# One core: batch 2's K transposed by TensorE, pairwise PV normalisation in tile 0, single banks in tile 1

## The chip, the core and the metric

The kernel runs on one core of a Trainium2 chip. A core has TensorE (PE in the profile; PEld is its weight load), VectorE (DVE), ScalarE (ACT), GpSimd (POOL) and SyncE (SP), each with an instruction queue of its own that is worked off in order, and 16 DMA engines that all of the core's transfers share. SP issues DMAs into a hardware queue (q1 in the profile), POOL into a software queue (q0). The metric is device time in microseconds (us); smaller is better.

## What is computed

Causal attention with a window of 64 positions over 8 batches, 8 heads, 576 positions, head dimension 64, and then a feed-forward block on the 4608 tokens:

```python
scores = scale * q @ k.T          # masked to 0 <= i - j < 64
attn = softmax(scores)
x = (attn @ v) as (4608, 512)     # tokens x (heads * head_dim)
h = x @ w_in                      # (4608, 2048)
g = h * clip(h + 3, 0, 6) / 6
out = g @ w_out                   # (4608, 512)
```

## The kernel before

**Tiles and stages.** The feed-forward part works on nine tiles of 512 tokens. Tile T has a stage 1 (`s1`, L524: 16 chunks of four 128x512 matmuls, L531, each chunk followed by `gate`, L536, which is a ScalarE activation, L538, and a VectorE product, L539) and a stage 2 (`s2`, L561: four output blocks of 16 matmuls, L568, a ScalarE copy to `osb`, L574, and a store). Tile T needs the attention output `xT` of batch T, because a batch has 576 tokens and a tile has 512; the last 64 positions of a batch are called its remainder.

**Attention of the next batch is woven into the stages.** Heads are taken in four pairs. `SS` (L630) computes the scores of a pair (ten small matmuls, L354, two exps on ScalarE, L362, one mask product on VectorE, L372). `N_` (L613) multiplies the probabilities with V, whose extra column of ones gives the sums (PV, L384 to L395), and VectorE divides head by head (L403 and L406). `X_` (L618) transposes the result into `xT` on TensorE and copies it with ScalarE (L422); `xt_dma` (L474) does the same with a DMA transpose on SP. `TT` (L621) transposes Q and K of a pair on TensorE, `RR` (L626) the remainder's. `rest_s`, `rest_n`, `rest_x` (L427 to L468) do attention of batch 0's remainder.

**The order is written out by hand.** `run` or `go` lets a stage go on by one block, and the calls between put attention work there. After stage 1 of tile 0, L760 to L798 interleave stage 2 of tile 0 (all four output blocks a quarter at a time, so that each quarter of w_out may land late) with batch 1's attention and batch 0's remainder. From tile 1 on `stage_` (L800) does it, with the tables that `pieces` (L820) returns: p1 holds what follows which chunk of stage 1, p2 what follows which block of stage 2. In tiles 1 and 2 stage 1 begins with four chunks held open, pair by pair, with the last two `X_` of the batch in between.

**PSUM** has eight banks: `st0` and `st1` of two banks each (scores, and other uses), `o`, `acc`, `h0` and `h1`. `s1_bank` (L494) says where a chunk of stage 1 goes. In tiles 1 and 2 the first four chunks take `st0` and `st1` as double banks with one gate over both halves.

**Loads.** Q, K and V of a batch pass a staging tile (`qst`, `kst`, `vst`, one buffer each), are cast to bf16 by POOL and then transposed. Batches 0 and 1 load Q and K in 1 KB runs (`LoadsForPE`, L101) and transpose on TensorE. Batches 2 to 7 load blocks of 256 B runs on SP (`load_blocks`, L88) and transpose by DMA on SP: batch 2 in eight transposes by pair (L280), the later ones in two whole ones (L272). The weights come on POOL's queue. V of batch 1 comes on SP, head by head (`load_v_by_head`, L121), made to wait for the third piece of w_out (L729). Casts and DMA issues of POOL stand in one order, L642 to L657 and L709 to L744 and L842 to L847. At most eight transfers of one queue are outstanding, since each issue waits for the landing of the eighth before it.

Of the kernel before, what the change touches and what calls it, by code (L numbers as in the profile page):

```python
# [9 lines left out]
F32 = mybir.dt.float32  # L10
# [14 lines left out]
def kernel(  # L25
# [53 lines left out]
    def load_v(b, vst, h0, h1):  # L79
        out = []  # L80
        for h in range(h0, h1):
            out.append(nc.sync.dma_start(
                out=vst[:, 0 : KB - 1, h, :],
                in_=v[b, h, 0:SM, :].rearrange("(k p) d -> p k d", p=P),
            ))
        return out

    def load_blocks(t, src, b, kbs, tail=0):  # L88
        out = []
        for kb in kbs:  # L90
# [3 lines left out]
            out.append(nc.sync.dma_start(  # L94
# [5 lines left out]
    class LoadsForPE:  # L100
        def __init__(self, b):  # L101
            self.b = b
            self.qst = stage.tile([P, H, R * D], F32, name="qst", tag="qst")
# [4 lines left out]
        def main(self, i, h0, h1):  # L108
            nc.gpsimd.dma_start(
# [4 lines left out]
        def rest(self):  # L114
            for i, src in enumerate((q, k)):
                nc.gpsimd.dma_start(
                    out=self.rst[i * SR : (i + 1) * SR, :, :],
# [3 lines left out]
    def load_v_by_head(b):  # L121
        vst = stage.tile([P, KB, H, D], F32, name="vst", tag="vst")
        ins = load_blocks(vst, v, b, (KB - 1,), SR) + load_v(b, vst, 0, H)
        return vst, ins

    def load_for_dma(b):
        sts, ins = [], []
        for n, src in (("qst", q), ("kst", k), ("vst", v)):
# [112 lines left out]
    class Batch:  # L241
# [28 lines left out]
        def transpose_by_dma(self):  # L270
            for n, T in ((qn_all, self.QT), (kn_all, self.KT)):
# [4 lines left out]

        def transpose_pairs_by_dma(self):
            for g in range(NG):
                for n, T in ((qn_all, self.QT), (kn_all, self.KT)):
                    nc.sync.dma_start_transpose(  # L280
                        out=T[:, g, :].rearrange("d (k s) -> d k s", s=P),
                        in_=n[:, g, :, :, :].rearrange("p k h d -> p (k h d)"),
                    )
# [8 lines left out]
        def cast_rest(self, st, copy):  # L292
            self.rn = consts.tile([P, H, D], BF16, name=f"rn{self.b}")
            copy(out=self.rn[:], in_=st[2][:])

        def rest_t(self, tr):
# [13 lines left out]
            return evac  # L310

# [100 lines left out]

    def xt_pe(bt, g, tr):
# [29 lines left out]
    def rest_n(bt, u):  # L443
# [8 lines left out]
        for h in range(2):  # L452
            ov = st[0:SR, h, 0 : NG * VW].rearrange("p (g w) -> p g w", w=VW)
            rec = small.tile([P, KB], F32, name="rec")
            nc.vector.reciprocal(out=rec[0:SR, 0:NG].unsqueeze(2), in_=ov[:, :, D:VW])
            nc.vector.tensor_tensor(
                out=opr[0:SR, :, h, :], in0=ov[:, :, 0:D],
# [433 lines left out]
```

## Time and profile before

| what | value |
|---|---|
| median of 8 runs | 313.96 us (313.03 to 314.9) |
| the profiled execution | 313.85 us |
| its span in the profile | 312.1 us |
| stage 1 of tile 0 starts at | 18.74 us |
| stage 2 of tile 0 starts at | 34.30 us |
| tiles 1, 2, 3 start at | 57.57, 91.70, 125.61 us |
| HBM read, written | 36.70 MB, 9.44 MB |

The span is the time from the first to the last instruction; some 1.75 us of the execution lie around it. The page has one row with each engine's busy time, 40 slices of the span, the DMA queues, the chain of work that ended last, and groups of instructions by line. The timeline lists an engine's instructions in order of time, with the idle time before each and what ended it in brackets. In the chain that ended last TensorE has the share to be seen here:

```profile
PE 86%; DMA 5%; DVE 3%; ACT 3%; issue 1%; SPq 1%; POOL 0%; POOLq 0%
```

### The profile page before, as it was taken

What the parts mean: (1) busy time and instruction counts of PE and PEld (TensorE: products, weight loads), DVE (VectorE), ACT (ScalarE), POOL (GpSimd) and SP (SyncE); (2) the same over time, 40 slices, a digit from 0 to 9 for tenths busy, and PEclk for the clock granted to TensorE, in tenths of its full rate; (3) what the DMA queues carried; (4) which work ended last, traced back from release to release, by engine and by line L of the source; (5) the groups of instructions that cost most, each with busy time, mean ns of one, the idle gap of its engine ahead of it and who ended that gap; (6) DMA issues with size and microseconds to landing.
All of it is one profiled execution on the core that took longest, in us unless ns stands there. A gap on an engine that the chain in (4) does not pass through costs nothing.

```text
span 312.1 us, 5616 instructions
## 1 busy us (share of the span) xinstructions
PE 302.2 (97%) x2162; PEld 148.2 (47%) x2162; DVE 174.7 (56%) x334; ACT 177.5 (57%) x264; POOL 92.9 (30%) x137
## 2 busy tenths in 40 slices
PE   8889998899999999999999999999999999999995
PEld 3445444544654455445544554455445544444442
DVE  4659546385636754578347844785377527306700
ACT  3848754587627853796169615871588157317611
POOL 5876615372055043415600660075000000000000
PEclk9999999999999999999999999999999999999999
DMA  7999999998899999999999999999900630010011
GB/s 248 209 220 241 245 200 205 206 244 174 187 205 213 266 201 213 220 227 210 191 250 199 203 192 245 213 206 187 250 3 0 129 93 0 34 69 34 0 69 67
DMA packets 147579, 52.80 MB, mean 169 GB/s; under 512 B 136384, under 2 KB 142528, under 8 KB 147552
## 3 DMA queue, kind: packets, MB, share of 16 engines
q1 hardware_dynamic: 141920, 44.18, 70.4%
q0 software_dynamic: 5360, 8.00, 12.7%
q8 instruction: 17, 0.28, 0.4%
q10 hardware_dynamic: 272, 0.26, 0.2%
q14 instruction: 10, 0.08, 0.1%
HBM read 36.70 MB, written 9.44 MB: 148 GB/s over the span
## 4 chain that ended last, share of the span: by engine, by line
PE 86%; DMA 5%; DVE 3%; ACT 3%; issue 1%; SPq 1%; POOL 0%; POOLq 0%
PE acc L568 19%; PE o L568 18%; PE h L531 17%; PE st L531 8%; PE o L531 6%; PE acc L531 6%; PE st L354 4%; DMA win<-in_moe_w_in_dram 2%; PE h L384 2%; DVE gT L539 2%; PE h L568 1%; DMA qst<-in_q_dram 1%; PE h L389 1%; ACT pT L362 1%; DMA vst<-in_v_dram 1%
## 5 line engine op out<-in xcount | busy, mean ns | idle before, releaser
L531 PEld LDWEIGHTS <-win 128*128 128x128 bf16 x576 | 55.1, 98 | 66.6 <-issue 1.6
L568 PEld LDWEIGHTS <-gT 128*128 128x128 bf16 x576 | 52.5, 98 | 57.0 <-issue 0.5
L568 PE MATMUL o<-wout,gT 128*128 128x512 bf16 x272 | 65.7, 380 | 0.0
L568 PE MATMUL acc<-wout,gT 128*128 128x512 bf16 x272 | 63.8, 379 | 0.0
L531 PE MATMUL h<-xT,win 128*128 128x512 bf16 x264 | 63.3, 379 | 0.0
L362 ACT ACTIVATE pT<-st 128x768 bf16<-128x768 f32 x64 | 48.8, 808 | 13.7 <-PE st L354 13.6
L539 DVE SCALAR_TENSOR_TENSOR gT<-t,st 128x512 bf16<-128x512 bf16 (+1 forms) x26 | 20.7, 810 | 57.2 <-ACT t L538 57.0
L538 ACT ACTIVATE t<-h,half 128x512 bf16<-128x512 f32 x66 | 44.7, 691 | 8.4 <-PE h L531 7.9
L539 DVE SCALAR_TENSOR_TENSOR gT<-t,h 128x512 bf16<-128x512 bf16 x66 | 44.6, 685 | 7.8 <-ACT t L538 7.7
L372 DVE TENSOR_TENSOR pT<-pT,mask 128x1536 bf16<-128x1536 bf16 x28 | 28.3, 1009 | 21.1 <-ACT pT L362 21.1
L258 POOL CAST qn<-qst 128x512 bf16<-128x512 f32 x24 | 15.9, 703 | 72.1 <-DMA qst<-in_q_dram 51.6
L574 ACT COPY osb<-acc 128x512 f32<-128x512 f32 x17 | 10.0, 587 | 42.8 <-PE acc L568 42.6
L531 PE MATMUL st<-xT,win 128*128 128x512 bf16 x128 | 30.9, 379 | 1.1 <-DMA win<-in_moe_w_in_dram 0.7
L574 ACT COPY osb<-o 128x512 f32<-128x512 f32 x17 | 10.0, 588 | 29.9 <-PE o L568 29.9
L406 DVE TENSOR_TENSOR opg<-h,rec 128x320 bf16<-128x320 f32 x50 | 24.6, 492 | 1.7
L531 PE MATMUL o<-xT,win 128*128 128x512 bf16 x92 | 23.6, 379 | 0.3 <-DVE gT L539 0.3
L538 ACT ACTIVATE t<-st,half 128x512 bf16<-128x512 f32 (+1 forms) x26 | 20.1, 785 | 6.3 <-PE st L531 6.2
L531 PE MATMUL acc<-xT,win 128*128 128x512 bf16 x92 | 23.6, 379 | 0.0
L248 POOL CAST V<-vst 128x512 bf16<-128x512 f32 (+1 forms) x14 | 16.6, 1185 | 16.6 <-DMA vst<-in_v_dram 10.6
L384 PEld LDWEIGHTS <-pT 128*128 128x128 bf16 x256 | 17.5, 97 | 7.8 <-DVE opg L406 0.9
L258 POOL CAST kn<-kst 128x512 bf16<-128x512 f32 x24 | 15.8, 699 | 17.0 <-DMA kst<-in_k_dram 14.1
L354 PE MATMUL st<-QT,KT 64*128 64x192 bf16 (+2 forms) x312 | 17.5, 230 | 0.9 <-ACT KT L322 0.5
(111 smaller groups left out, 282.8 us busy)
## 6 DMA issues: line engine op xcount, KB each, us to landing
out_dram<-osb SPq DMA_DIRECT2D x32, 256.0 KB, 2.5
qst<-in_q_dram SPq DMA_DIRECT2D x28, 256.0 KB, 4.8
kst<-in_k_dram SPq DMA_DIRECT2D x27, 256.0 KB, 5.4
vst<-in_v_dram SPq DMA_DIRECT2D x24, 256.0 KB, 5.6
vst<-in_v_dram SPq DMA_DIRECT2D x23, 128.0 KB, 3.9
win<-in_moe_w_in_dram POOLq DMA_DIRECT2D x4, 512.0 KB, 8.4
wout<-in_moe_w_out_dram POOLq DMA_DIRECT2D x4, 512.0 KB, 12.6
qst<-in_q_dram POOLq DMA_DIRECT2D x2, 512.0 KB, 11.7
```

The lines of the kernel that those rows point to most:

```text
L248: copy(out=self.V[:, 0 : KB - 1, h0:h1, 0:D], in_=vst[:, 0 : KB - 1, h0:h1, :])
L258: pcopy(out=n[:, g, 0 : KB - 1, :, :].rearrange("p k h d -> p k (h d)"), in_=s[:, 0 : KB - 1, 2 * g : 2 * g + 2, :].rearrange("p k h d -> ...
L354: nc.tensor.matmul(st[:, h, o0 : o0 + n], lhsT=bt.KT[h * D : (h + 1) * D, g, k0 : k0 + P], rhs=bt.QT[h * D : (h + 1) * D, g, q0 : q0 + n], ...
L362: nc.scalar.activation(out=pT[:, :, 2 * u : 2 * u + 2, 0:QW], in_=st[:, :, 0:w].rearrange("p h (k w) -> p h k w", k=2), func=EXP, scale=scale,
L372: nc.vector.tensor_tensor(out=pT[:, :, :, 0:QW], in0=pT[:, :, :, 0:QW], in1=mask[:].rearrange("p (h k) w -> p h k w", h=2), op=MULT,)
L384: nc.tensor.matmul(ob, lhsT=pT[:, h, qb, 0:P], rhs=V[:, qb, 2 * g + h, :], start=True, stop=(qb == 0),)
L406: nc.vector.tensor_tensor(out=opgs[bt.b, g][:, 0:nb, h, :], in0=ov[:, :, 0:D], in1=rec[:, 0:nb].unsqueeze(2).to_broadcast([P, nb, D]), op= ...
L531: nc.tensor.matmul(hT, lhsT=win16[:, g, fc * P : (fc + 1) * P], rhs=xT[:, g, t0 : t0 + TB], start=(g == 0), stop=(g == NG - 1),)
L538: nc.scalar.activation(out=t1[:], in_=hT, func=RELU, bias=half[:], scale=1.0 / 6.0)
L539: nc.vector.scalar_tensor_tensor(out=out, in0=t1[:], scalar=1.0, in1=hT, op0=MIN, op1=MULT,)
L568: nc.tensor.matmul(accs[ts], lhsT=gT[:, fc, ts * P : (ts + 1) * P], rhs=wout16[:, fc, :], start=(fc == 0), stop=(fc == NFC - 1),)
L574: acopy(out=osb[:], in_=accs[ts])
```

## The change

What it does, part by part:

- **Q and K of batch 2.** Q is loaded as before in 256 B runs, then transposed by one whole DMA transpose. K is loaded in 1 KB runs by SP, in two transfers and one for the remainder, cast by POOL and transposed by TensorE in tile 1: pairs 0, 1, 2 after chunks 10, 12, 14 of stage 1, pair 3 and the remainder (`rest_tk`) after the first two blocks of stage 2. The eight DMA transposes by pair go.
- **V of batch 1** is loaded by POOL's queue instead of SP's, and its explicit wait for w_out goes. Q of batch 2 waits for V's third head instead.
- **Batch 1's remainder** of Q and K is loaded before the first piece of w_out, cast before the second and third, and transposed on TensorE before the last chunk of tile 0's stage 1.
- **Tile 0's stage 2** is ordered anew: both halves of a pair's scores together and earlier, PV of the four pairs at the end in `st0` and `st1` in turn, each pair normalised by one reciprocal and one product (`pv_pair`; the remainder likewise). Batch 0's remainder of Q and K is cast by VectorE and that of V by ScalarE, not by POOL.
- **Stage 1 of tile 1** takes single banks in turn out of six (`turn`), with one gate per chunk from the first on. Tile 2 keeps its double banks for four chunks and takes other banks after them.
- **Batch 3** gets `xT` by DMA transposes like the later batches, not by `X_`. Its casts and transposes are moved in the tables, and its scores start three chunks earlier.

The diff, cut to its core:

```diff
+        def __init__(self, b, eng):
+            self.b, self.eng = b, eng
+            self.qst = None if b > 1 else stage.tile([P, H, R * D], F32, name="qst", tag="qst")
...
-            nc.gpsimd.dma_start(
+            self.eng.dma_start(
...
+        def rest(self, which=(0, 1)):
+            for p, i in enumerate(which):
+                src = (q, k)[i]
+                self.eng.dma_start(
+                    out=self.rst[p * SR : (p + 1) * SR, :, :],
...
-        ins = load_blocks(vst, v, b, (KB - 1,), SR) + load_v(b, vst, 0, H)
+        ins = load_blocks(vst, v, b, (KB - 1,), SR, nc.gpsimd) + load_v(b, vst, 0, H, nc.gpsimd)
...
+        def rest_tk(self, tr):
+
+            for g in range(NG):
+                nc.tensor.transpose(
+                    out=tr[:, g * SR : (g + 1) * SR],
+                    in_=self.rn[0:SR, 2 * g : 2 * g + 2, :].rearrange("p h d -> p (h d)"),
+                    identity=ident[0:SR, 0:SR],
+                )
+            acopy(
+                out=self.KT[:, :, SM:S], in_=tr[:, 0 : NG * SR].rearrange("d (g s) -> d g s", s=SR),
+            )
 
         def main_t(self, g, i, tr, copy=None):
 
@@ -410,6 +417,19 @@
 
         return norm
 
+    def pv_pair(bt, g, u):
+        t = ps_st.tile([P, 2, 512], F32, name=f"st{u}")
+        for h in range(2):
+            pv(bt, g, h, t[:, h, :])
+        ov = t[:, :, 0 : KB * VW].rearrange("p h (k w) -> p h k w", w=VW)
+        rec = small.tile([P, 2, KB], F32, name="rec2")
+        nc.vector.reciprocal(out=rec[:].unsqueeze(3), in_=ov[:, :, :, D:VW])
+        opgs[bt.b, g] = opool.tile([P, KB, 2, D], BF16, name="opg")
+        nc.vector.tensor_tensor(
+            out=opgs[bt.b, g][:].rearrange("p k h d -> p h k d"), in0=ov[:, :, :, 0:D],
+            in1=rec[:].unsqueeze(3).to_broadcast([P, 2, KB, D]), op=MULT,
+        )
...
-        for h in range(2):
-            ov = st[0:SR, h, 0 : NG * VW].rearrange("p (g w) -> p g w", w=VW)
-            rec = small.tile([P, KB], F32, name="rec")
-            nc.vector.reciprocal(out=rec[0:SR, 0:NG].unsqueeze(2), in_=ov[:, :, D:VW])
-            nc.vector.tensor_tensor(
-                out=opr[0:SR, :, h, :], in0=ov[:, :, 0:D],
-                in1=rec[0:SR, 0:NG].unsqueeze(2).to_broadcast([SR, NG, D]), op=MULT,
-            )
-
-    def rest_x(bt, u):
-        tr = ps_st.tile([P, 2, 1024], BF16, name=f"st{u}")[:, 0, :]
+        ov = st[0:SR, :, 0 : NG * VW].rearrange("p h (g w) -> p h g w", w=VW)
+        rec = small.tile([P, 2, KB], F32, name="rec2")
+        rec = rec[0:SR, :, 0:NG]
+        nc.vector.reciprocal(out=rec.unsqueeze(3), in_=ov[:, :, :, D:VW])
+        nc.vector.tensor_tensor(
+            out=opr[0:SR].rearrange("p g h d -> p h g d"), in0=ov[:, :, :, 0:D],
+            in1=rec.unsqueeze(3).to_broadcast([SR, 2, NG, D]), op=MULT,
+        )
+
+    def rest_x(bt, tr):
...
+        if T == 1:
+            return turn()
+        if T == 2:
+            if fc in (8, 9):
+                return ps_st.tile([P, 2, 512], F32, name=f"st{fc % 2}")[:, 0, :]
+            if fc in (6, 7, 12, 13):
+                return (ps_o, ps_acc)[fc % 2].tile([P, 512], F32, name=("o", "acc")[fc % 2])[:]
+            return h_bank()[:]
...
+    def turn(tr=False):
+        i = turns[0] % 6
+        turns[0] += 1
+        shape, dt = ([P, 1024], BF16) if tr else ([P, 512], F32)
+        if i < 2:
+            return ps_h.tile(shape, dt, name=h_name())[:]
+        if i < 4:
+            return (ps_o, ps_acc)[i - 2].tile(shape, dt, name=("o", "acc")[i - 2])[:]
+        return ps_st.tile([P, 2, shape[1]], dt, name=f"st{i - 4}")[:, 0, :]
...
+        if T == 1:
+            hTs = [turn() for fc in range(4)]
+            for gs in first:
+                for fc in range(4):
+                    mms(fc, hTs[fc], gs)
+                yield
+            for fc in range(4):
+                mms(fc, hTs[fc], (NG - 1,))
+                gate(gT[:, fc, :], hTs[fc], [P, TB])
+                yield
+        elif first:
...
+    ld = LoadsForPE(1, nc.gpsimd)
     ld.main(0, 0, 4)
     ld.main(1, 0, 4)
     w_in.append(load_w_in(1536, 2048, 0, NG))
+    ld.rest()
     w_out = [load_w_out(0, 4)]
...
-    ld.rest()
     ld.main(0, 4, 8)
     ld.main(1, 4, 8)
...
+    bt.cast_rest(st, pcopy)
     w_out += [load_w_out(4 * i, 4 * i + 4) for i in (1, 2)]
     rst0, rvst0 = load_rest_of_first()
+    cast_pairs(bt, st, 4, 4)
     w_out.append(load_w_out(12, 16))
     vst1, insv = load_v_by_head(1)
-    for x in insv:
-        after(x, w_out[2], "the weights go first")
-    bt.cast_rest(st, pcopy)
-    cast_pairs(bt, st, 4, 4)
-    bt0.cast_rest((None, None, rst0), pcopy)
-    run(m, 11)
+    run(m, 12)
     TT(bt, 0, oa_tr)
     run(m, 2)
     TT(bt, 1, oa_tr)
+
+    def st_tr(u):
+        t = ps_st.tile([P, 2, 1024], BF16, name=f"st{u}")
+        return iter((t[:, 0, :], t[:, 1, :]))
+
+    run(m, 1)
+    RR(bt, st_tr(0))
     run(m)
 
-    pcopy(out=bt0.V[SR:P, KB - 1, :, 0:D], in_=rvst0[SR:P, :, :])
     bt.cast_v_end(vst1, pcopy)
     for g in range(NG):
         bt.cast_v(vst1, 2 * g, 2 * g + 2, pcopy)
-    st2, _ = load_for_dma(2)
-
...
+    st2, ins2 = load_for_dma(2, (0,))
+    after(ins2[0], insv[3], "the values go first")
+    ld = LoadsForPE(2, nc.sync)
+    ld.main(1, 0, 4)
+    ld.main(1, 4, 8)
+    ld.rest((1,))
...
-    S1_(0, 0, 0)
-    S1_(1, 0, 1)
+    def SS1_(g):
+        S1_(g, 0, 0)
+        S1_(g, 1, 1)
+
+    go()
+    SS1_(0)
     go(2)
-    RR(bt, st_tr(0))
+    SS1_(1)
     go()
-    S1_(0, 1, 1)
+    TT(bt, 2, st_tr(0))
     go()
-    S1_(1, 1, 0)
-    TT(bt, 2, st_tr(1))
+    TT(bt, 3, st_tr(1))
     go(2)
-    TT(bt, 3, st_tr(0))
+    SS1_(2)
+    go(3)
+    bt0.cast_rest((None, None, rst0), vcopy)
+    RR(bt0, st_tr(0))
     go()
-    S1_(2, 0, 1)
+    SS1_(3)
+    acopy(out=bt0.V[SR:P, KB - 1, :, 0:D], in_=rvst0[SR:P, :, :])
+    go(2)
+    rest_s(bt0, 0)
+    go(2)
+    rest_n(bt0, 1)
+    pv_pair(bt, 0, 0)
     go()
-    S1_(2, 1, 0)
-    go()
-    S1_(3, 0, 1)
-    go()
-    S1_(3, 1, 0)
-    go()
-    RR(bt0, st_tr(1))
-    go()
-    rest_s(bt0, 0)
-    go()
-    rest_n(bt0, 1)
-    go()
-    N_(bt, 0, st_pair(0))
-    go()
-    N_(bt, 1, oa)
-    rest_x(bt0, 0)
-    go()
-    two = st_tr(1)
-    X_(bt, 0, two)
-    X_(bt, 1, two)
-    N_(bt, 2, oa)
-    N_(bt, 3)
+    pv_pair(bt, 1, 1)
+    X_(bt, 0, oa_tr)
+    rest_x(bt0, next(oa_tr))
+    pv_pair(bt, 2, 0)
+    pv_pair(bt, 3, 1)
+    X_(bt, 1, st_tr(0))
 
...
-            X_(Batch(T), 2, oa_tr)
+            X_(Batch(T), 2, oa_tr if T == 2 else st_tr(0))
             run(m, 1)
-            X_(Batch(T), 3, oa_tr)
+            X_(Batch(T), 3, oa_tr if T == 2 else st_tr(1))
...
-            return p1, {
-                1: [f(SS, 0)], 2: [f(SS, 1)], 4: [f(N_, 0), f(SS, 2)], 6: [f(X_, 0)], 7: [f(N_, 1), f(SS, 3)],
-                9: [f(X_, 1)], 11: [f(N_, 2)], 13: [f(N_, 3)],
-            }
-        if bt.b == 3:
-            return {13: [f(SS, 0)]}, {
-                0: [f(SS, 1)], 3: [f(N_, 0), f(SS, 2)], 5: [f(X_, 0)], 6: [f(N_, 1), f(SS, 3)],
-                8: [f(X_, 1)], 9: [f(N_, 2)], 11: [f(X_, 2)], 12: [f(N_, 3)], 14: [f(X_, 3)],
+            def k_t(g, tr, copy):
+                return lambda: bt.main_t(g, 1, tr() if tr else turn(True), copy)()
+
+            return {
+                10: [k_t(0, None, acopy)], 12: [k_t(1, None, vcopy)], 14: [k_t(2, None, acopy)],
+            }, {
+                0: [k_t(3, h_tr, vcopy)], 1: [lambda: bt.rest_tk(h_tr())],
+                2: [f(SS, 0)], 4: [f(SS, 1)], 6: [f(N_, 0), f(SS, 2)], 8: [f(N_, 1), f(SS, 3)],
+                9: [f(X_, 0)], 11: [f(N_, 2)], 12: [f(X_, 1)], 14: [f(N_, 3)],
             }
...
-    bt2.cast_for_dma(st2, (0, 1))
+    bt2.cast_for_dma((*st2, None), (0,))
+    vst2 = stage.tile([P, KB, H, D], F32, name="vst", tag="vst")
+    load_blocks(vst2, v, 2, range(3), SR)
+    bt2.transpose_by_dma((0,))
+    load_blocks(vst2, v, 2, range(3, KB), SR)
+    for h in (0, 4):
+        bt2.cast_qk(ld.tiles, 1, h, 4, pcopy)
+    bt2.cast_rest(ld.tiles, pcopy, SR)
     for u0, osb in held:
         nc.gpsimd.dma_start(out=out[u0 : u0 + P, :], in_=osb[:])
-    bt2.cast_for_dma(st2, (2,))
-    bt2.transpose_pairs_by_dma()
+    bt2.cast_for_dma((None, None, vst2), (2,))
...
+            (p2 if T == 1 else p1).setdefault(6, []).append(
                 lambda bt=nxt, sts=sts: bt.cast_for_dma(sts)
             )
-            p2.setdefault(6 if T < 3 else 12, []).append(lambda bt=nxt: bt.transpose_by_dma())
+            p2.setdefault(8 if T == 1 else 12, []).append(lambda bt=nxt: bt.transpose_by_dma())
...
```

## The prediction

> **What bounds the kernel now.** I read the page's busy row first, then its slices, then a table of stages cut at each tile's first matmul, then the matmul timeline inside the stages that stand out.
>
> ```profile
> PE 302.2 (97%) x2162; PEld 148.2 (47%) x2162; DVE 174.7 (56%) x334; ACT 177.5 (57%) x264; POOL 92.9 (30%) x137
> PEclk9999999999999999999999999999999999999999
> DMA  7999999998899999999999999999900630010011
> ```
>
> TensorE is busy 97% of 312.1 us at full granted clock, so time goes away only where TensorE waits or has less to do. The DMA engines are full until about 230 us, so each moved transfer needs its landing checked.
>
> ```profile
> 34.30:57.57 23.27, 21.44 (x217) 11.23 (x215) 11.64 (x26) 12.57 (x20) 9.96 (x18) 1.00 1.19 205
> 57.57:72.83 15.26, 14.85 (x80) 6.65 (x77) 10.94 (x19) 10.72 (x15) 10.23 (x16) 1.00 1.22 228
> 91.70:107.10 15.40, 15.10 (x85) 7.10 (x84) 8.87 (x12) 11.91 (x18) 5.98 (x8) 1.00 1.10 235
> 107.10:125.61 18.51, 18.51 (x179) 10.43 (x178) 10.16 (x22) 9.82 (x16) 7.17 (x11) 1.00 1.15 205
> 125.61:157.40 31.79, 31.79 (x234) 15.63 (x233) 19.34 (x36) 18.53 (x28) 12.48 (x16) 1.00 1.15 214
> 253.00:280.60 27.60, 27.60 (x130) 12.48 (x129) 11.01 (x16) 13.34 (x20) 0.00 (x0) 1.00 0.11 40
> ```
>
> Columns: stretch, its length, then busy PE, PEld, DVE, ACT, POOL. The stretches are stage 2 of tile 0, stage 1 of tile 1, stages 1 and 2 of tile 2, tile 3, tile 7. A tile without attention takes 27.60 (13.8 a stage); one with a batch's attention and xT by DMA 31.79. Tile 1 takes 57.57 to 91.70, 34.13; tile 2 33.91. The first row holds 13.8 of matmuls and about 6.4 of attention, counted from row pitches: scores 0.54 a pair (0.44 of them issued before 34.30), PV 0.49 a pair, four transposes 0.22, five 0.28, the remainder's three steps 0.8. That is 20.2 of 23.27: **3.1 us of waits** (modelled matmul ends hide part of them from the busy column). The timeline of TensorE shows the largest, with the releaser in brackets:
>
> ```profile
> 49.02 0.29 PE L431 MATMUL st<-QT,KT 64*128 64x64 bf16 x8 [0.57 <-DVE KT L308]
> 50.51 0.44 PE L448 MATMUL st<-V,pTr 128*64 128x65 bf16 x8 [0.23 <-DVE pTr L438]
> 56.32 0.44 PE L417 MATMUL st<-ident,opg 128*128 128x128 bf16 x5 [0.94 <-ACT xT L422]
> 63.93 2.15 PE L531 MATMUL st<-xT,win 128*128 128x512 bf16 x8 [0.30 <-DVE gT L539]
> ```
>
> **Tile 0's tail.** The batch-1 remainder transpose (0.22) moves ahead of the last stage-1 chunk, so stage 2 begins 0.22 later relative to 33.86, where TensorE leaves stage 1 now: 34.1. It needs `rn`, which POOL casts after the two 128 KB loads that now go before `w_out`. w_in's last piece lands at 29.6; the two loads took 1.6 together behind w_out's first piece (32.3 to 33.9), so 31.2, cast by 31.9, wanted at 33.0. w_out's first piece moves back by the same 1.6 to 33.9, wanted at 34.1: covered by 0.2. Pieces two and three are issued behind that cast, 31.9 instead of 27.9, while the queue is occupied until 36.7; they still land near 39.05 and 41.8, against 39.4 and 45 wanted.
>
> The walk, TensorE's clock in us: block 35.0; score pair 0 waits until ScalarE frees its bank from the remainder's K copy (35.3), 35.85; two blocks and pair 1, 38.1; block and transposes of pair 2, 39.4; block, pair 3's, 40.75; two blocks and score pair 2, 43.0; three blocks, 45.6. Batch 0's remainder cast now stands on DVE behind the mask product: ScalarE's two exps end at 44.4, the mask (1.0) at 45.4, the cast at 46.0. No row has this cast; DVE's 128x256 and 128x512 copies take 0.29 and 0.68, POOL's same cast 0.62; I take 0.6. Wait 0.4. Remainder transpose and block, 47.1; score pair 3, two blocks, 49.4; remainder scores and two blocks, 51.35. Both waits shown at 49.02 and 50.51 are covered by these blocks. Remainder PV, 51.7; PV 0, 52.2; block, 53.1; PV 1, 53.55.
>
> Here DVE sets the pace. It now normalises a pair at once. Its rows:
>
> ```profile
> 52.45 0.20 DVE L403 RECIPROCAL rec<-st 128x5 f32<-128x5 f32 x1 [0.29 <-PE st L395]
> 52.67 0.49 DVE L406 TENSOR_TENSOR opg<-st,rec 128x320 bf16<-128x320 f32 x1
> 51.19 0.42 DVE L456 TENSOR_TENSOR opr<-st,rec 64x256 bf16<-64x256 f32 x1
> ```
>
> From 256 to 320 elements costs 0.07, so 640 cost 0.84 and, with 0.21 for the reciprocal, a pair 1.0 instead of 1.28. Remainder done at 52.7, pair 0 53.75, pair 1 54.75. The xT transposes of pair 0 follow at 53.85 to 54.1, remainder transpose 54.35, PV 2 54.85, PV 3 55.35. Those of pair 1 now sit in score bank 0, which DVE is still reading for pair 2 until 55.9: they run 56.0 to 56.3. So a DVE release takes the place of the 0.94 on ScalarE. Tile 1 starts at 56.3 instead of 57.57: **-1.3**.
>
> V of batch 1 leaves SP (nine issues, 41.90 to 49.3) for POOL, behind w_out's last piece (its issue moves from 34.33 to about 37.9, lands 46.2, wanted 48.5). Nine POOL issues at the 0.71 of the `rst` loads are 6.4 us; two wait for landings at 46.2 and 46.9. POOL's casts of V queue behind them, and batch 2's Q loads on SP wait for V's third head.
>
> The Trainium skill speaks against this: "DMA: Bandwidth & Descriptors", section "SWDGE vs HWDGE vs iDMA", gives plain transfers to SP or ACT and only casting or irregular ones to GpSimd. Its row on SP: now the last V cast runs at 51.81. On POOL the nearest row is `rst`, 128 KB in 256 B runs, whose landings lie 0.5 to 1.1 apart; I take 0.8, as SP's 256 B blocks arrive (256 KB every 1.1 to 1.4) and the full engines price both alike. Fourth item (V's third head) at 49, Q's first bytes 1.7 later, then both queues share. In 66 to 72 us the software queue's out stores took 53% of the engines' time beside SP's 60%, so about half each: nine loads end near 55.0, last cast 56, which would move PV 3 from 54.85 to 56 and the start of tile 1 by 0.5. The same page, "Queues, rings and completion order", says that an engine alternates between queues by whole packets; here those were 4 KB in the software queue and 256 B in SP's, which gives POOL's V nearly all: end near 53.4, cast 54.4, nothing lost. From 43 to 44 us, with V already moving on SP's queue, the software queue did write 176 packets of w_out where 200 a microsecond were its quiet rate. I take nothing, and keep +0.5 in the range.
>
> **Tile 1.** Stage 1 took 15.26 where matmuls and two xT groups need 14.4: 0.9 lost, the 0.30 shown at 63.93 among it, because double-bank gates (ACT 1.1, DVE 1.3) release two banks at once. Six single banks leave 5.2 us between uses of one against a gate of about 1.5: I take -0.8. K of batch 2 on TensorE adds 3 x 0.22 here, 0.7 with switches, and 0.4 in stage 2 (pair 3, remainder); the evacuations fit, ACT and DVE being idle 30%. Stage 2's one wait of 0.2, scores on ScalarE's bank, goes as scores are spread out. Together **+0.1**.
>
> Its inputs: K is two loads of 512 KB in 1 KB runs plus one of 128 KB instead of five of 256 B runs; POOL's 1 KB loads landed 1.5 apart, so about 60 to 61. POOL casts Q by 61.3 and K by 63.4, wanted at 66.4. SP's eight pair transposes (66.18 to 78.16) become one (3.5 in the 96.27 row): issued near 62, landed by 69 even with the first one's 6.9, wanted at 74.5. V, behind it, lands by 70, wanted at 80. Batch 3's loads begin near 66 instead of 78.21, so its transposes (96.27 to 102.6 now) land near 93, wanted at 100. POOL's held out stores and casts follow the same order, earlier. All this is nothing on the path.
>
> **Tile 2.** Batch 3's four xT groups leave TensorE: 4 x 0.28 = -1.1. Their transposes on SP (two in 2.58) end some 1.5 before tile 3 needs them; tile 4 lives with less. Chunks 8 and 9 in score banks spare the 0.30 wait on DVE at 99.66. **-1.4**. Later tiles are unchanged.
>
> Sum: -1.3 + 0.1 - 1.4 = -2.6 from the profiled execution's 313.85 (312.1 of span, 1.75 around it): **311.3**. That execution is 0.11 below the median of 313.96.
>
> **Rivals.** (a) V of batch 1 comes late (0.20). Speaks for it: 256 B runs on a busy software queue, Q's loads released early on another. With 1.1 per load from 46.2, Q's data from 52.3 and half shares, V ends at 59.9, cast 60.9, tile 1 at 61.7: +4.1 + 0.1 - 1.4 = +2.8, 316.7. It beats the gain once the last cast ends after about 58.3. Against: it takes the slow end of both rows. (b) Waits only change place (0.18): DVE's chain and w_out's thin 0.2 cover eat tile 0's gain to -0.3, the new K transposes stall the banks so that tile 1 costs +0.7, tile 2 gives -1.2: 313.0. (c) The waits I counted in tile 0 (0.3, 0.4, 0.65) mostly vanish, since a bank frees sooner or the DVE cast takes 0.3: -1.2 more, 310.1 (0.17). Main case 0.45, own range 310.6 to 312.2. The compiled order does hold these moves, with equal TensorE instruction counts, so a change without effect is left out.
>
> Measurement tells apart about 0.3%, 0.94 us: faster means under 312.9, slower over 314.8. Faster: 0.45 + 0.17 + 0.05 of (b) = 0.67; same 0.13 of (b) + 0.02 of (a) = 0.15; slower 0.18. The range 309.7 to 314.2 holds all but (a)'s upper part.
>
> **What would show it.** Tile 1's first matmul near 56.3, pair 1's xT transposes before it released by DVE; no wait on POOL's V at PV 3; stage 1 of tile 1 at 15.1; tile 2 near 32.5 without xT transposes; SP's first batch-3 load near 66. Wrong if TensorE waits for V, w_out or `rn` before tile 1, or if tile 2 stays above 33.3.

## The result and the profile after

| | before | after |
|---|---|---|
| median | 314.11 us (312.76 to 315.35, 32 runs) | 311.58 us (310.94 to 311.94, 11 runs) |
| profiled execution, span | 313.85, 312.14 us | 311.58, 309.55 us |

The changed kernel takes 0.9918 of the time of the one before, with a 95% interval of 0.9903 to 0.9934. The forecast was 311.3.

The busy row and the DMA slices of the page after the change:

```profile
PE 301.8 (98%) x2162; PEld 148.7 (48%) x2162; DVE 174.8 (56%) x329; ACT 176.0 (57%) x266; POOL 100.1 (32%) x142
DMA  7999998999999999999999999999900630010011
```

TensorE has as many instructions and as much work as before (301.8 against 302.2 us); the span is 2.6 us shorter. So nearly all that went is time in which TensorE had nothing to do. Where it went is read from stretches cut at each tile's first matmul. The columns are those of the table in the prediction: stretch, length, busy PE, PEld, DVE, ACT, POOL, granted clock, DMA share, GB/s. The rows are stage 2 of tile 0, stages 1 and 2 of tile 1, stages 1 and 2 of tile 2.

```profile
33.59:56.07 22.48, 21.45 (x219) 11.67 (x218) 12.45 (x23) 12.38 (x20) 15.95 (x24) 1.00 1.05 205
56.07:71.16 15.09, 15.09 (x90) 7.49 (x87) 10.31 (x17) 12.12 (x20) 7.55 (x12) 1.00 1.17 239
71.16:90.20 19.04, 19.04 (x187) 10.45 (x186) 10.43 (x23) 10.03 (x16) 10.07 (x13) 1.00 1.17 206
90.20:106.30 16.10, 15.74 (x96) 7.46 (x95) 9.92 (x14) 13.16 (x20) 3.66 (x4) 1.00 1.16 234
106.30:123.33 17.03, 17.00 (x149) 8.82 (x148) 9.47 (x21) 5.85 (x10) 9.50 (x13) 1.00 1.09 202
```

| stretch | before | forecast | after | gain forecast | gain measured |
|---|---|---|---|---|---|
| up to tile 1's start | 57.57 | 56.3 | 56.07 | -1.3 | -1.5 |
| tile 1 | 34.13 | about 34.2 | 34.13 | +0.1 | 0.0 |
| tile 2 | 33.91 | about 32.5 | 33.13 | -1.4 | -0.78 |
| tile 3 to the end | 186.53 | 186.5 | 186.21 | 0 | -0.3 |

The busy share of tile 1's stage 1 shows what single banks did: 15.09 of 15.09 us, where 14.85 of 15.26 was busy before, although three K transposes were added. Tile 2's stage 1 is the only row after tile 0 with a visible idle part (15.74 of 16.10).

The timeline of TensorE of the changed kernel gives the waits that are left before tile 3. Each line is start, duration, line, output and inputs, and in brackets the idle time and what ended it:

```profile
34.77 0.51 PE L361 MATMUL st<-QT,KT 64*128 64x192 bf16 x10 [0.15 <-ACT KT L303]
45.39 0.40 PE L294 MATMUL st<-ident,rn 128*128 128x128 bf16 x4 [0.24 <-DVE rn L289]
55.78 0.45 PE L437 MATMUL st<-ident,opg 128*128 128x128 bf16 x5 [0.58 <-DVE opg L428]
101.15 0.34 PE L361 MATMUL st<-QT,KT 64*128 64x192 bf16 x6 [0.26 <-DVE gT L572]
```

The first three are the three that the prediction's walk through tile 0 named, each where and for the reason it named. The fourth it did not have.

How far one profile carries: in seven profiled executions in which TensorE's work in tile 0 is that of the changed kernel (the changed kernel, its repeat and five of the experiments below), tile 1 started at 55.37 to 56.68 us (mean 56.1). Most of the spread is there before tile 0 begins (its stage 1 starts at 17.55 to 18.76). In six executions with an unchanged tile 2 that tile took 32.94 to 33.23 (mean 33.06).

### The profile page after: what moved, and what is told of

Its sections match the earlier page's. It is cut to its first block, busy times and chain, and to the rows that moved or that the text cites. A ratio compares the mean times of both kernels' runs of the same rounds, so it can differ in the third digit from the quotient of the medians.

```text
span 309.5 us, 5607 instructions
## 1 busy us (share of the span) xinstructions
PE 301.8 (98%) x2162; PEld 148.7 (48%) x2162; DVE 174.8 (56%) x329; ACT 176.0 (57%) x266; POOL 100.1 (32%) x142
## 4 chain that ended last, share of the span: by engine, by line
PE 91%; DVE 5%; ACT 2%; DMA 1%; issue 1%; POOL 0%
PE o L611 19%; PE acc L611 19%; PE h L564 18%; PE st L564 8%; PE acc L564 6%; PE o L564 6%; PE st L361 5%; DVE gT L572 2%; PE h L391 2%; PE h L611 2%; PE h L396 1%; DMA qst<-in_q_dram 1%; ACT pT L369 1%; PE h L324 1%; PE st L349 1%
## 5 line engine op out<-in xcount | busy, mean ns | idle before, releaser
L564 PE MATMUL h<-xT,win 128*128 128x512 bf16 x268 | 65.0, 379 | 0.0
L572 DVE SCALAR_TENSOR_TENSOR gT<-t,st 128x512 bf16<-128x512 bf16 (+1 forms) x26 | 19.5, 768 | 55.5 <-ACT t L571 55.4
L260 POOL CAST qn<-qst 128x512 bf16<-128x512 f32 x24 | 17.2, 756 | 62.3 <-DMA qst<-in_q_dram 60.0
L564 PE MATMUL st<-xT,win 128*128 128x512 bf16 x120 | 28.7, 379 | 0.0
L564 PE MATMUL acc<-xT,win 128*128 128x512 bf16 x96 | 25.1, 379 | 0.0
L413 DVE TENSOR_TENSOR opg<-h,rec 128x320 bf16<-128x320 f32 x48 | 23.6, 492 | 1.7
L571 ACT ACTIVATE t<-st,half 128x512 bf16<-128x512 f32 (+1 forms) x26 | 19.3, 755 | 5.1 <-PE st L564 4.6
L571 ACT ACTIVATE t<-acc,half 128x512 bf16<-128x512 f32 x24 | 16.5, 688 | 3.9 <-PE acc L564 3.2
L361 PEld LDWEIGHTS <-KT 64*128 64x128 bf16 x312 | 11.2, 94 | 15.3 <-issue 12.4
```

What stands on the lines that cost most here:

```text
L260: pcopy(out=n[:, g, 0 : KB - 1, :, :].rearrange("p k h d -> p k (h d)"), in_=s[:, 0 : KB - 1, 2 * g : 2 * g + 2, :].rearrange("p k h d -> ...
L361: nc.tensor.matmul(st[:, h, o0 : o0 + n], lhsT=bt.KT[h * D : (h + 1) * D, g, k0 : k0 + P], rhs=bt.QT[h * D : (h + 1) * D, g, q0 : q0 + n], ...
L413: nc.vector.tensor_tensor(out=opgs[bt.b, g][:, 0:nb, h, :], in0=ov[:, :, 0:D], in1=rec[:, 0:nb].unsqueeze(2).to_broadcast([P, nb, D]), op= ...
L564: nc.tensor.matmul(hT, lhsT=win16[:, g, fc * P : (fc + 1) * P], rhs=xT[:, g, t0 : t0 + TB], start=(g == 0), stop=(g == NG - 1),)
L571: nc.scalar.activation(out=t1[:], in_=hT, func=RELU, bias=half[:], scale=1.0 / 6.0)
L572: nc.vector.scalar_tensor_tensor(out=out, in0=t1[:], scalar=1.0, in1=hT, op0=MIN, op1=MULT,)
```

## The experiments

Ratios are to the kernel before, in runs on the same chip. Times by stage come from each kernel's profile. Except where another base is named, an edit is made to the changed kernel.

**Batch 3's transposes back on TensorE.** The table of tile 2 gets four `X_`, with nothing else moved:

```diff
+        if bt.b == 3:
+            return p1, {
+                0: [f(SS, 2)], 1: [f(N_, 0)], 2: [f(SS, 3)], 3: [f(N_, 1)], 5: [f(X_, 0)], 6: [f(N_, 2)],
+                7: [f(X_, 1)], 8: [f(N_, 3)], 10: [f(X_, 2)], 11: [f(X_, 3)],
+            }
```

> The changed kernel, with batch 3's xT transposed by TensorE again (four groups of five 128x128 transposes in stage 2 of tile 2, each with its ScalarE copy) and not by DMA. My sum (the gain of tile 2 is TensorE instructions that left): stage 2 of tile 2 grows from 17.03 us by 4 x 0.28 = 1.1 to about 18.1, nothing else moves, the whole is about 1.1 us slower than the changed kernel (near 312.7). Rival (the DMA transposes cost tile 3 a hidden wait, so that the move is worth little): tile 3 gets shorter than 31.67 and the whole changes by under 0.5 us.

313.83 us, 0.9959 [0.9924, 0.9995]. Stage 2 of tile 2, by its stretch in this profile:

```profile
106.11:124.14 18.03, 18.03 (x170) 9.80 (x168) 9.13 (x21) 8.21 (x14) 9.40 (x12) 1.00 0.86 176
```

It is 1.0 us longer than the 17.03 above, with 21 more recorded matmuls, and tile 3's stage 1 stays at 14.90. So the four groups were worth what their instructions take, and the DMA transposes that stand for them delayed nothing here.

**One product per head in tile 0** (`pv_pair` keeps its banks, its order and all else):

```diff
-        nc.vector.reciprocal(out=rec[:].unsqueeze(3), in_=ov[:, :, :, D:VW])
-        nc.vector.tensor_tensor(
-            out=opgs[bt.b, g][:].rearrange("p k h d -> p h k d"), in0=ov[:, :, :, 0:D],
...
+        for h in range(2):
+            nc.vector.reciprocal(out=rec[:].unsqueeze(2), in_=ov[:, h, :, D:VW])
+            nc.vector.tensor_tensor(
+                out=opgs[bt.b, g][:, :, h, :], in0=ov[:, h, :, 0:D],
...
```

> The changed kernel, with the PV results of tile 0's tail normalised head by head (eight reciprocals and eight products on VectorE) and all else as changed. My reading (VectorE's release of score bank 0 sets the start of tile 1): a pair costs VectorE 1.26 us instead of 1.0, pair 2 ends some 0.5 to 0.8 us later, the xT transposes of pair 1 wait 0.3 to 0.8 longer than the 0.58 seen, and tile 1 starts that much later than 56.07. Rival (another wait, V or the exps, ends last there): tile 1 starts within 0.1 us of 56.07.

312.86 us, 0.9927 [0.9901, 0.9953], too near the changed kernel's own ratio to tell from it by time alone. The profile tells more. Stage 2 of tile 0 took 23.11 instead of 22.48 us, and TensorE's timeline there has two waits on VectorE's products where the changed kernel has one of 0.58:

```profile
54.70 0.45 PE L438 MATMUL o<-ident,opg 128*128 128x128 bf16 x5 [0.32 <-DVE opg L429]
57.41 0.45 PE L438 MATMUL st<-ident,opg 128*128 128x128 bf16 x5 [0.71 <-DVE opg L429]
```

The waits grew by 0.45, the stage by 0.6. VectorE's pace over four pairs does set the end of tile 0.

**V of batch 1 back on SP's queue**, with its wait for w_out:

```diff
-        ins = load_blocks(vst, v, b, (KB - 1,), SR, nc.gpsimd) + load_v(b, vst, 0, H, nc.gpsimd)
+        ins = load_blocks(vst, v, b, (KB - 1,), SR) + load_v(b, vst, 0, H)
...
+    for x in insv:
+        after(x, w_out[2], "the weights go first")
...
-    after(ins2[0], insv[3], "the values go first")
```

> The changed kernel, with V of batch 1 loaded on SP's queue again behind the third piece of w_out, as before the change, and Q of batch 2 behind it on the same queue. My reading (the queue of V is worth nothing, as its casts end before PV needs them on either): the last V cast begins near 51.8 instead of 52.63, tile 1 starts within 0.2 us of 56.07, the whole within 0.3 us of the changed kernel. Rival (POOL's queue matters: V on SP pushes batch 2's loads or comes late): a wait on POOL's V ahead of PV, or tile 1 or 2 longer by 0.5 us or more.

311.51 us, 0.9881 [0.9857, 0.9906]; tile 1 starts at 56.41, and the other six of the seven executions above span 55.37 to 56.68. The queue that V takes makes no difference that these runs can tell.

**K of batch 2 by DMA again**, in 256 B runs and eight transposes by pair, with batch 3's `xT` still by DMA:

```diff
-    st2, ins2 = load_for_dma(2, (0,))
+    st2, ins2 = load_for_dma(2)
...
-    ld = LoadsForPE(2, nc.sync)
...
+    for g in range(NG):
+        for n, T in ((qn_all, bt2.QT), (kn_all, bt2.KT)):
+            nc.sync.dma_start_transpose(
...
-                10: [k_t(0, None, acopy)], 12: [k_t(1, None, vcopy)], 14: [k_t(2, None, acopy)],
...
```

> The changed kernel, with K of batch 2 loaded in 256 B runs and Q and K transposed by eight DMA transposes of pairs again, so that TensorE is rid of the 20 K transposes. By TensorE's instructions alone it would be 1.1 us faster (5 groups near 0.22). My reading (the K transposes buy time on SP and the DMA engines for batch 3): SP's loads of batch 3 start some 8 to 10 us later than 69.5, its xT transposes come after tile 3 needs them or its Q and K after the scores, and the whole is 1 us or more slower than the changed kernel, with a wait at the scores of batch 3 or at the start of tile 3. Rival (SP has slack enough): no such wait, about 1 us faster.

319.36 us, 1.0148 [1.0122, 1.0174]. Tile 1 gained little and tile 2 lost far more. The timeline of TensorE in this kernel, at the end of tile 1's stage 1 and in stage 1 of tile 2:

```profile
71.63 2.75 PE L611 MATMUL o<-wout,gT 128*128 128x512 bf16 x12 [0.64 <-DVE gT L572]
...
106.80 0.82 PE L361 MATMUL st<-QT,KT 64*128 64x192 bf16 x10 [6.44 <-DMA KT<-kn]
```

The scores of batch 3 wait 6.4 us for its K. On SP, batch 3's loads started at 78.48 us instead of 69.53, and its K transpose was issued at 102.42 instead of 94.13: 8.3 us later, of which some 2 had been slack. In tile 1 itself K on TensorE costs 0.42 us: stage 2 is 18.49 without it and 19.04 with it, but stage 1 is 15.22 without it and 15.09 with it, since there its transposes stand in time in which TensorE otherwise waits for the last gate (the 0.64 above). Its worth is the 9 us that it takes off SP's queue. (The loads at 69.53 are in the changed kernel's timeline of SP, quoted below.)

**Batch 3's transposes by DMA alone**, on the kernel before (its `X_` of batch 3 become `xt_dma`; batch 4's Q and K transposes move to the end of tile 2's stage 2):

```diff
-                0: [f(SS, 1)], 3: [f(N_, 0), f(SS, 2)], 5: [f(X_, 0)], 6: [f(N_, 1), f(SS, 3)],
-                8: [f(X_, 1)], 9: [f(N_, 2)], 11: [f(X_, 2)], 12: [f(N_, 3)], 14: [f(X_, 3)],
+                0: [f(SS, 1)], 3: [f(N_, 0), f(SS, 2)], 5: [f(xt_dma, 0)], 6: [f(N_, 1), f(SS, 3)],
+                8: [f(xt_dma, 1)], 9: [f(N_, 2)], 11: [f(xt_dma, 2)], 12: [f(N_, 3)], 14: [f(xt_dma, 3)],
```

> The kernel before, with only batch 3's xT by DMA transposes (each in the place of the xT group it replaces, and batch 4's Q and K transposes after them). By TensorE's instructions alone: 1.1 us faster than before, near 313.0. My reading (without the relief of SP the transposes stand behind batch 4's loads, which SP issues until 121.7 us): the four transposes go out between about 122 and 129 us, the last lands near 131, tile 3 waits several us for it, and the whole is 3 to 5 us slower than before, 317 to 319. Rival (SP is early enough): faster by 1 us.

322.04 us, 1.0224 [1.0195, 1.0253], worse than expected. On SP the four transposes were issued between 125.5 and 132.0 us, behind batch 4's loads (in the changed kernel between 115.95 and 121.9). TensorE's timeline as tile 3 begins:

```profile
129.42 0.38 PE L531 MATMUL st<-xT,win 128*128 128x512 bf16 x1 [2.24 <-DMA xT<-opg]
130.59 0.38 PE L531 MATMUL st<-xT,win 128*128 128x512 bf16 x1 [0.80 <-DMA xT<-opg]
132.11 0.58 PE L531 MATMUL st<-xT,win 128*128 128x512 bf16 x1 [1.14 <-DMA xT<-opg]
133.48 2.29 PE L531 MATMUL st<-xT,win 128*128 128x512 bf16 x5 [0.79 <-DMA xT<-opg]
```

Four waits make 5.0 us. Tile 3's stage 1 took 20.52 us instead of 14.90; only 2.7 us of these waits lie inside it. The other 2.9 us are shown by the stretches of this kernel, in which the third number from the end is the granted clock:

```profile
130.00:133.40 3.40, 0.96 (x2) 0.20 (x2) 0.00 (x0) 0.00 (x0) 1.16 (x2) 0.67 0.77 185
133.40:138.00 4.60, 4.52 (x11) 1.62 (x11) 1.38 (x2) 1.85 (x3) 0.00 (x0) 0.50 1.21 216
138.00:140.00 2.00, 2.00 (x10) 0.88 (x9) 1.28 (x2) 1.34 (x3) 0.00 (x0) 1.00 1.13 253
```

From 133.4 to 138 TensorE hardly waited and got through 11 matmuls at half clock, where the 2 us after them held 10. The expectation counted the waits and not the clock after them.

**Scores of tile 2 two chunks later**, after the late gates:

```diff
-        p1 = {10: [f(SS, 0)], 13: [f(SS, 1)]}
+        p1 = {12: [f(SS, 0)], 14: [f(SS, 1)]} if bt.b == 3 else {10: [f(SS, 0)], 13: [f(SS, 1)]}
```

> The changed kernel, with batch 3's first two score pairs put after chunks 12 and 14 of tile 2's stage 1 instead of after 10 and 13. My reading of the missing 0.6 us in tile 2 (score pair 0 waits for the gates of chunks 8 and 9, which the change put into the score banks, while VectorE is still behind after the two double gates): the wait of 0.26 us on VectorE at 101.15 goes, stage 1 of tile 2 falls from 16.10 to between 15.5 and 15.8, the whole gains 0.3 to 0.6 us. Rival (the double banks at the start of the stage hold TensorE up wherever the scores stand): stage 1 stays within 0.1 us of 16.10, with the wait on another bank.

311.94 us, 0.9902 [0.9865, 0.9938]. Stage 1 of tile 2 fell from 16.10 to 15.49, and stage 2 rose from 17.03 to 17.54. In the timeline of this kernel the wait stands a few matmuls further on:

```profile
109.51 0.22 PE L391 MATMUL h<-V,pT 128*128 128x65 bf16 x2 [0.43 <-DVE gT L572]
```

ScalarE now has the exps of two pairs close behind each other among the last gates, and PV of pair 0 waits for the bank of a late gate. The cause of the 0.6 was right; this edit only moves it.

**Pair 1's last transposes of tile 0 in bank `o`** instead of a score bank, so that they need not wait for pair 2's product:

```diff
-    X_(bt, 1, st_tr(0))
+    X_(bt, 1, oa_tr)
```

> The changed kernel, with the xT transposes of pair 1 at the end of tile 0 in bank o instead of score bank 0. My reading (they wait 0.58 us only because VectorE still reads score bank 0 for pair 2): they follow PV 3 at once, near 54.8 instead of 55.78, and tile 1 starts 0.6 to 1.0 us earlier than 56.07, of which the third chunk's wait for bank o may take back 0.3; the whole gains 0.4 to 0.9 us. Rival (the next thing, pair 2's or 3's normalisation ahead of its own xT transposes, is as late): stage 1 of tile 1 grows by as much and the whole changes by under 0.2 us.

312.86 us, 0.9936 [0.9914, 0.9958]: by time no gain over the changed kernel is seen (its repeat on this chip, below, has 311.59), and 0.4 to 0.9 us was expected. The start was late in its profile (19.69 us), so it is read by stages. Stage 2 of tile 0 fell to 21.81, 0.67 less than in the changed kernel, and stage 1 of tile 1 rose from 15.09 to 15.53:

```profile
57.42 0.38 PE L564 MATMUL o<-xT,win 128*128 128x512 bf16 x1 [0.51 <-ACT xT L442]
```

The third chunk of tile 1 comes to bank `o` while ScalarE still copies the transposes out of it. Two thirds of the gain is a wait that changes its place.

**Double banks in tile 1**, on the kernel just shown (the last two `X_` of the batch go from the score banks back to `o` and `acc` with it):

```diff
-        if T == 1:
+        if False:
             hTs = [turn() for fc in range(4)]
...
-            X_(Batch(T), 2, oa_tr if T == 2 else st_tr(0))
+            X_(Batch(T), 2, oa_tr)
...
```

> The kernel of h_x1_o, with stage 1 of tile 1 begun in the two double banks with one gate over both halves, as before the change (the later chunks keep the six banks in turn). My sum (single banks are worth 0.8 us of waits): stage 1 of tile 1 is 0.5 to 0.9 us longer than in h_x1_o, with a wait on VectorE or ScalarE at its fifth to ninth chunk. Rival (six banks in turn after the fourth chunk take the wait by themselves): less than 0.2 us longer.

313.97 us, 0.9973 [0.9944, 1.0002] (the profiled execution, 317.31, is the slowest of its ten: its tile 0 starts late, at 19.62, and stage 1 of tile 0 takes 17.80 us at a granted clock of 0.84; the edit touches neither). Stage 1 of tile 1, at a clock of 1.00, took 17.20 us instead of 15.53, more than expected; the medians are 1.1 apart. TensorE's timeline has three waits for it:

```profile
59.74 0.38 PE L564 MATMUL st<-xT,win 128*128 128x512 bf16 x1 [0.39 <-DVE rec L426]
60.64 0.60 PE L564 MATMUL st<-xT,win 128*128 128x512 bf16 x2 [0.52 <-DVE opg L428]
76.94 1.02 PE L611 MATMUL o<-wout,gT 128*128 128x512 bf16 x4 [1.50 <-DVE gT L572]
```

The first two are the score banks, which VectorE still normalises when tile 1 wants them both. The third is the last gates; why they come so late was not tried. The new tail of tile 0 thus needs the single banks of tile 1: `pv_pair` occupies the very banks with which the old stage 1 began. Single banks with the old tail were not run.

**The changed kernel again, single banks in tile 2, and both bank edits together**, on one chip. The second gives tile 2's first four chunks single banks and its last `X_` the score banks, so that the score banks are used last by chunks 4 and 5:

```diff
-        if T == 1:
-            hTs = [turn() for fc in range(4)]
+        if T in (1, 2):
+            hTs = [turn() if T == 1 else s1_bank(fc, T) for fc in range(4)]
...
-            if fc in (8, 9):
+            if fc in (4, 5):
                 return ps_st.tile([P, 2, 512], F32, name=f"st{fc % 2}")[:, 0, :]
-            if fc in (6, 7, 12, 13):
+            if fc in (2, 3, 8, 9, 12, 13):
```

The third adds the edit in bank `o` to it, with tile 1's third and fourth banks exchanged (`acc` first, then `o`).

> The changed kernel itself, on the same chip as the two next ones, as their measure. Both theories: 0.990 to 0.993 of the kernel before; stage 1 and 2 of tile 2 at 16.1 and 17.0 us, tile 0's stage 2 within 0.4 us of 22.5.

> The changed kernel, with stage 1 of tile 2 begun in four single banks (h0, h1, o, acc) with a gate per chunk, chunks 4 and 5 in the score banks, and the score pairs left after chunks 10 and 13. My reading (the missing 0.6 us of tile 2 comes from VectorE's late double gates, which leave the score banks of chunks 8 and 9 unreleased when score pair 0 comes): stage 1 of tile 2 falls from 16.09 to 15.4 to 15.6 us and stage 2 stays at 17.0, the whole gains 0.5 to 0.7 us. Rival (ScalarE and VectorE lack time in that stretch, so that a wait only moves on, as when the scores were put later): stage 1 falls but stage 2 grows by as much, under 0.2 us in all.

> The kernel of i_t2_single, and with it the xT transposes of pair 1 in bank o, where that bank is the fourth of tile 1's six and no longer the third, so that ScalarE has one matmul more to empty it. My reading: tile 0's stage 2 is 0.6 us shorter than in the changed kernel, stage 1 of tile 1 at 15.1 to 15.3 instead of the 15.52 with bank o third; the whole is 1.0 to 1.3 us faster than the changed kernel, 0.987 to 0.989 of the kernel before. Rival: the wait on ScalarE's copy of pair 1 stays at 0.4 to 0.5 us whichever chunk meets it, as the second pass needs that xT as well; then 0.7 us in all.

| kernel | median (range, runs) | ratio to before | stage 2 of tile 0 | stage 1 of tile 1 | tile 2 | stage 1 of tile 3 |
|---|---|---|---|---|---|---|
| changed, again | 311.59 (310.89 to 312.45, 10) | 0.9906 [0.9871, 0.9940] | 22.84 | 15.09 | 32.94 | 14.90 |
| single banks in tile 2 | 311.64 (310.13 to 314.07, 12) | 0.9913 [0.9885, 0.9940] | 22.59 | 15.09 | 32.63 | 14.90 |
| both edits | 310.86 (310.6 to 311.4, 6) | 0.9896 [0.9865, 0.9927] | 21.78 | 15.30 | 32.64 | 15.60 |

In the second kernel the wait at the scores of tile 2 is gone, and stage 1 is 15.77 us there instead of 16.09, where 15.4 to 15.6 was expected. The median does not show these 0.3 us. A new wait stands at the stage's start, in no bracket of TensorE's timeline, but in the pitch of its matmuls:

```profile
89.51 0.89 PE L564 MATMUL h<-xT,win 128*128 128x512 bf16 x2
90.23 0.38 PE L564 MATMUL o<-xT,win 128*128 128x512 bf16 x1
```

The first two matmuls take 0.72 us up to the third, where 0.43 is usual. The second of them opens the second chunk in an `h` bank that VectorE reads until 89.94 for the last PV product of the tile before, and the timeline of the weight loads (PEld) has an idle time of 0.53 there, ended by that product. The third kernel has the same delay. The third brings the tail of tile 0 down by 0.8 to 1.1 against the other two, for 0.21 in tile 1; in all it gains less than the expected 1.0 to 1.3. Its timeline shows one more wait:

```profile
123.55 1.24 PE L564 MATMUL st<-xT,win 128*128 128x512 bf16 x5 [0.54 <-DMA xT<-opg]
```

Tile 2 ends before the DMA transposes of its own batch have landed. SP issued the last two of them 2.6 us before tile 3 began, in the second kernel, with the same tile 2 and no wait, 4.9 us. The third kernel's median is 0.7 us below the changed kernel's, but the intervals overlap; that it is the faster one is likely and not settled.

## Why the prediction was right, and which term was off

The sum of -2.6 was met to 0.1 us (the span fell by 2.59), and that is partly luck: tile 2 fell short by 0.6, and an earlier start of tile 0 and shorter later tiles, which nothing here traces to the change, made up for it.

**Tile 0, -1.3: right in its waits; its size is helped by an early start.** The three waits that the walk named are in the trace, at 0.15, 0.24 and 0.58 where 0.3, 0.4 and 0.65 were put. VectorE's cast of the remainder, for which there was no row, took 0.59 (0.6 taken), and a pair's product 0.82 (0.84 from the two smaller rows). That VectorE sets the pace there is shown by the run with one product per head. Tile 1 starts at 56.07 where 56.3 was worked out, but stage 2 of tile 0 is not shorter than the walk had it: 22.48 us where 22.2 was counted (34.1 to 56.3). It began at 33.59 and not at 34.1, 0.4 of this by an earlier start of tile 0, which varied by more than that between executions of the same code. By its two stages alone tile 0 took 38.83 us before (38.44 in the run with batch 3's transposes alone, which has the old tile 0) and 37.65 to 38.48, mean 38.05, in the seven executions: 0.4 to 0.8 us by the mean, 1.1 in the profile that was read. The medians' 2.5 less tile 2's 0.86 and the later tiles' 0.2 to 0.3 leave 1.4, with the start in it.

**V on POOL's queue: nothing, as taken, but not by the reasoning.** The row-based reading had the last cast of V at 56; with the Trainium skill's rule that an engine takes turns between queues by whole packets ("DMA: Bandwidth & Descriptors", "Queues, rings and completion order") it was 54.4. The timeline of POOL in the changed kernel:

```profile
47.32 0.75 POOL L82 DMA_DIRECT2D vst<-in_v_dram  x1 [0.33 <-DMA vst<-in_v_dram]
52.63 0.63 POOL L250 CAST V<-vst 128x512 bf16<-128x512 f32 x1
53.32 0.29 POOL L252 CAST V<-vst 64x128 bf16<-64x128 f32 x1
```

The last cast ends at 53.6. From 48.11 us on POOL's casts stand one behind the other with no wait for data, so this end is POOL's own pace of issues and casts. SP issued Q's loads from 48.67 on, but the software queue moved its last packets between 50 and 51 us, and SP's queue had moved only 0.03 MB in the microsecond before. So the two queues hardly shared the engines, V had landed by 51, some 2 us before the better of the two readings (53.4), and no run here tests the rule. The same page's section "SWDGE vs HWDGE vs iDMA", which gives plain transfers to SP or ACT, made no difference that the runs can measure. Rival (a), V late, is out.

**Tile 1, +0.1: borne out as a sum** (0.0), and stage 1 is 15.09 where 15.1 was written, without a wait. Its terms were both too large and cancel. K on TensorE was put at +1.1 and costs 0.42, since its transposes fill the wait for the last gate. So single banks and the scores' new places, with all else that changed in tile 1, bring 0.4 over before (34.13 to the 33.71 of the kernel without K on TensorE), where -1.0 was put. That the old double banks cost 1.7 in the new order need not contradict this: there the new tail of tile 0 still holds the score banks.

**Tile 2, -1.4: the mis-sized term** (-0.78; -0.86 with the mean of six executions). It was made of two. The -1.1 for four xT groups held: 1.0 in the first experiment. The failed step is "Chunks 8 and 9 in score banks spare the 0.30 wait on DVE". Counted by stages: stage 1 should have taken 15.40, plus 0.54 for the score pair that moved into it, minus 0.30, 15.64; it took 16.10. Stage 2 should have given up 0.54 and 1.1, 16.87; it took 17.03, and 16.85 in the second profile. So the miss lies in stage 1. The wait of 0.30 did go. But the scores start three chunks earlier, after chunk 10, and want `st0` and `st1` while the gates of chunks 8 and 9 still hold them. The blocks ahead of the scores and behind them, in the changed kernel and then in the one with single banks in tile 2, which has no wait there:

```profile
99.42 1.03 PE L564 MATMUL h<-xT,win 128*128 128x512 bf16 x4
101.42 1.04 PE L564 MATMUL h<-xT,win 128*128 128x512 bf16 x4
...
99.01 1.03 PE L564 MATMUL h<-xT,win 128*128 128x512 bf16 x4
100.41 1.04 PE L564 MATMUL h<-xT,win 128*128 128x512 bf16 x4
```

From the one block to the other 2.00 us pass in the first and 1.40 in the second: 0.6 us lost in place of 0.3. The run with later scores got these 0.6 out of stage 1, and the one with single banks only 0.3, since it came to this point 0.3 later (9.50 us after the stage's start against 9.22), by the new wait for an `h` bank shown above. The step looked at which bank a chunk frees and not at who wants it next.

**Later tiles, 0: -0.3 measured**, 186.53 to 186.21. Nine other executions with the same code from tile 3 on have 186.04 to 186.56, so the one value before lies within their spread, and no gain is shown.

**"Nothing on the path" for SP: right in sum, and too light in what it said.** Batch 3's loads were to begin near 66 and Q's one transpose to take 3.5, with 6.9 allowed for. The timeline of SP in the changed kernel has

```profile
60.99 7.18 SPq L275 DMA_TRANSPOSE QT<-qn  x1
68.22 1.26 SPq L94 DMA_DIRECT2D vst<-in_v_dram  x2
69.53 6.33 SPq L94 DMA_DIRECT2D qst<-in_q_dram  x5
```

7.18 us for the transpose (4.7 to 6.9 in seven other executions), and 69.53 for the loads. What draws the transpose out was not tried. The cover took it: nobody waits for batch 3's K. But the sum priced K's move and the DMA transposes of `xT` as two parts, and they are one. Without K's move the scores of batch 3 wait 6.4 us; with the DMA transposes alone tile 3 waits 5.0. The "some 1.5" by which the transposes were to be early is no fixed margin. In nine executions without a wait the last two were issued 3.6 to 6.1 us before tile 3 began, 4.0 in the changed kernel's profile; in the kernel with both bank edits it was 2.6, and TensorE waited 0.54. By these two numbers some 3.1 us are needed, an estimate, which leaves 0.4 to 3.0 to spare.

**Rivals.** (b), waits that only change place, was right in tile 2 and in both bank edits. Its other half, w_out's thin cover of 0.2, came true in three of the seven executions, though not in the one that was read: TensorE waits for w_out in stage 2 of tile 0 for 0.18 us, for 0.39, and in the repeat of the changed kernel for 0.23 and 0.33. These three have the longest stage 2 of tile 0, 22.82 to 22.86 us, against 22.30 to 22.59 in the other four. The prediction had named such a wait as a sign that it is wrong. The waits take 0.2 to 0.6 us of tile 0's gain and not all of it. (c), the tail's waits gone, did not come: 0.97 us of the 1.35 that were counted stayed.

## What to carry to other kernels

Work that is moved off a DMA queue is priced by what stands behind it in that queue: here transposing K on TensorE saved tile 1 nothing and cost it 0.42 us, and it paid because the next batch's loads began 9 us earlier. When a bank is given to a chunk, look at the next user of that bank and the gate in between; sparing one wait of 0.3 brought one of 0.6 because its next user had been moved ahead. Check parts of a change in pairs, since one alone may cost more (+7 us here) than all of them together gain.

## What the hardware did that was not expected

In two runs a stretch of waits cost TensorE more than its length. With batch 3's transposes by DMA alone, 5.0 us of waits had three lone matmuls between them. The granted clock was down to 0.50 from 132 us on, when two of the three had run, and stayed there until 138, and tile 3's first stage lost 2.9 us beyond its waits. With K by DMA, after the single wait of 6.44 us, the stretches from 106 us on show it:

```profile
106.00:110.00 4.00, 3.07 (x15) 1.46 (x17) 0.96 (x1) 2.03 (x3) 0.00 (x0) 0.50 1.16 276
110.00:114.00 4.00, 3.92 (x25) 1.82 (x25) 2.08 (x4) 2.99 (x6) 0.27 (x1) 0.92 1.34 209
```

The length of a wait alone does not decide it. Behind the wait of 1.50 in the kernel with double banks the clock stayed at 1.00. But in the same execution it was at 0.50 from 18.5 to 25 us, beginning within a wait of 1.95 us for the first weights and less than 1 us after TensorE's last matmul, and stage 1 of tile 0 lost some 2 us by it. The kernel with pair 1's transposes in bank `o` had a wait of 1.93 at the same place, and its clock stayed at 1.00. The Trainium skill ("TensorE: Matmul & The Clock Gate", "Part 1: The HAM clock gate (the "warmup" mystery)") has half clock after an idle window of about 3.4 us and full clock after as much work. The wait of 6.44 us agrees with it: the last matmul ended at 100.36, the clock was 1.00 up to 103 and 0.50 from 104; work began again at 106.80, and the clock was 1.00 from 111. The first run shows that two lone matmuls in the idle stretch did not keep the clock up. The fall at 18.5 us came sooner than such a window, and its cause stays open.
